# First layer of a feed-forward block as seven block products for five more token chunks, with the whole schedule laid anew

## The chip, the cores and the metric

The kernel runs on one core of a Trainium2 chip. The core has a matrix engine (PE, with its own row for weight loads, PEld), a vector engine (DVE), a scalar engine for exp, log and copies (ACT), a general engine (POOL) which here mostly issues loads, and SP, which issues stores and DMA transposes. Each engine gets its own list of instructions, in the order in which the kernel issues them; between engines semaphores make one wait for another. In this kernel PE's results go to banks of PSUM, from which ACT and DVE read; all other tiles lie in SBUF. The metric is device time in microseconds from start to end of one launch.

## The reference

Attention with 8 heads over 4 batches of 768 positions, head size 64, followed by a feed-forward block on the 3072 x 512 result:

```python
scores = scale * np.matmul(q, k.transpose(0, 1, 3, 2)) + bias     # bias = -slope * distance
scores = np.where(is_global | is_local, scores, -1e9)             # 8 global keys, 96 local ones
a = softmax(scores)
x = (a @ v).transpose(0, 2, 1, 3).reshape(3072, 512)
h = x @ w_in                                                      # 512 -> 2048, layer 1
g = np.maximum(h, 0.0) + np.log1p(np.exp(-np.abs(h)))             # softplus
return g @ w_out                                                  # 2048 -> 512, layer 2
```

The output is float32, 3072 x 512.

## The kernel before

Tokens are worked in 24 blocks of 128 (six a batch) for attention and in 12 chunks of 256 (two blocks each) for the feed-forward block. A block needs, for the local window, its own keys and those of the block before it; the eight global keys are copied into the unused rows of the latter (`gk`, `gv`).

For a block n the steps are: loads of q, k and v on POOL's queue, which cast to bf16 (`lq`, `lk`, `lv`); transposes of q and k, in the first blocks on PE with copies out of PSUM (`t`, `qc`, `kc`), from block 8 on by DMA from SP's queue (`d`); scores (`s`, or `ss` for both halves of the heads); the bias added on DVE (`ab`, `ac`; in the first blocks by a matmul, `z`); exp on ACT (`e`); PV (`p`); division by the sum on DVE (`nm`); transposition of the result (`x` with its copy `xc`, or `y` by DMA), which gives `XT`, the input of layer 1.

Layer 1 of a chunk c has two forms. In the direct one, for chunks 0 to 6, it is eight units `f`, numbered 8c + u, each of two output blocks of 128 features and four contraction steps, that is eight matmuls of 128 x 128 by 256 columns (`ffn1`, L429), into one of three rotating PSUM banks. ACT takes an exp of each unit (`fe`, `soft`, L440), and a log of 1 + that for two units together (`lp`, `plus`, L448), which gives G, the input of layer 2.

In the other form, for chunks 7 to 11, the product is split in two along features in, features out and tokens, and made of seven block products instead of eight (Strassen, in Winograd's arrangement). Each half u of the blocks runs through: product 1 into bank "x" (`h`, `h_prod`, L536, eight matmuls by 128 columns); a copy of x into bank "y" (`hc` 1, `h_copy`, L546); product 2 added into y, which is output quarter 11; product 5 into bank "z", copied to SBUF as `hp` (`hc` 5, L549); product 6 added into x; z = hp + x on DVE (`hv` 6, `h_sum`, L561); product 3 added into z, quarter 12; product 7 added into x; quarter 22 = hp + x, on DVE into SBUF (`hv` 7); product 4 added into x, quarter 21. Each quarter then gets its exp (`he`, `h_exp`, L566), each half of the features its log (`hl`, `h_plus`, L570). The differences of the input are made on DVE (`ht`, `x_dif`, L507), the sums of the weights once, in eight parts (`hw`, `w_sum_part`, L480 to L490). Between product 1 and the last exps such a unit holds three banks, x, y and z.

The same three banks, b0, b1 and b2, serve the transposes on PE and half of the scores (`s_lo`); which of them each user gets stands in the string BANKS. The other banks are fixed: two for scores, one for PV, two for layer 2.

Layer 2 of chunks 1 to 11 is made of seven block products too (`m`, `prod`, L652), eight matmuls by 256 columns each, with sums of G on DVE (`gs`, L622) and copies and sums out of PSUM (`ec`, L681; `ev`, L691). Chunk 0 has it direct (`o`, L581). Stores (`st`) go by SP's queue.

What sets the order of all work is written out by hand: the string ORDER lists every step once, and a loop calls them in that order, so each engine, each DMA queue and each PSUM bank gets its work as the string has it. Steps of the kind `g` (L700) are copies of one element of G on POOL, which hold back the loads behind them until that part of G is there. `w18` is nine matmuls on constants at the start.

```python
    for name in ORDER.split():
        kind = name.rstrip("0123456789.")
        KINDS[kind](*(int(i) for i in name[len(kind) :].split(".")))
```

## Time and profile before

| what | value |
|---|---|
| timed runs | 203.88, 204.22, 205.57 us; median 204.22 |
| profiled execution, first to last instruction (span) | 201.9 us |
| median of the timed runs above that span | 2.3 us |
| PE busy | 195.3 us, 97% |
| weight loads (PEld) busy | 166.9 us, 83% |
| DVE busy | 163.6 us, 81% |
| ACT busy | 163.4 us, 81% |
| POOL busy | 77.0 us, 38% |
| granted TensorE clock | 1.000 |
| direct layer 1: matmuls | 448, mean 273 ns |
| seven-product layer 1: matmuls | 560, mean 219 ns |

The page gives the profiled execution by its span alone; its own time beside the span is not among the records, so the median of the timed runs stands in the table. A group's row has its line, engine, operation, output and inputs, shapes and count, then the busy time and the mean of one, then the idle time of the engine just before and what ended it. Matmuls overlap: the mean of one is its latency, and how many fit into a stretch is seen from start to start in the timeline. The slices of the page are 40 equal parts of the span, each about 5 us.

### The profile page before, as it was taken

Reading aid. Unit: us, or ns where it says so; the run is one execution under the profiler, and the core shown is the slowest. Engines: PE = TensorE matmul, PEld = TensorE weight load, DVE = VectorE, ACT = ScalarE, POOL = GpSimd, SP = SyncE. Lnnn points to the kernel's source line nnn. Section 1 sums busy time; section 2 is a strip of 40 time slices with the busy share of each in tenths; the row PEclk is TensorE's granted clock in tenths of the full one; section 3 lists DMA queues with packets and bytes.
Section 4 is the critical chain, followed back from the end, with each engine's and each line's share of the span. In section 5 each row is a group of like instructions: output and inputs, shape, how many; then the busy total and the mean of one; then the engine's idle time right before and its main releaser. Section 6 shows DMA issues by size and latency. Waiting matters only on the chain.

```text
span 201.9 us, 6147 instructions
## 1 busy us (share of the span) xinstructions
PE 195.3 (97%) x2487; PEld 166.9 (83%) x2489; DVE 163.6 (81%) x392; ACT 163.4 (81%) x253; POOL 77.0 (38%) x119
## 2 busy tenths in 40 slices
PE   7899999999999999999999998999999999999993
...
DVE  7765479589999988787889989999999986888541
ACT  2976899936599799687897998999999898999410
...
PEclk9999999999999999999999999999999999999999
...
GB/s 129 152 169 175 162 190 191 205 164 151 169 116 126 134 204 110 148 143 127 133 193 161 197 89 155 154 141 160 162 117 108 29 52 81 0 109 0 3 208 104
DMA packets 110619, 26.87 MB, mean 133 GB/s; under 512 B 101760, under 2 KB 108288, under 8 KB 110592
## 3 DMA queue, kind: packets, MB, share of 16 engines
...
q10 hardware_dynamic: 1040, 0.26, 0.6%
...
## 4 chain that ended last, share of the span: by engine, by line
PE 79%; DMA 7%; ACT 6%; DVE 5%; issue 1%; DVEq 0%; ACTq 0%
PE o L652 28%; PE hT L429 23%; PE hT L536 8%; PE x_ps L375 4%; PE s_ps L279 3%; PE o L581 3%; DMA out_dram<-osb 3%; PE p_ps L536 3%; ACT Pb L359 3%; DMA k_f<-in_k_dram 2%; DMA XT<-xsf 2%; PE tr L222 2%; ACT e_sb L566 2%; PE s_lo L279 1%; ACT G L570 1%
## 5 line engine op out<-in xcount | busy, mean ns | idle before, releaser
L429 PE MATMUL hT<-XT,w_in 128*128 128x256 f16 x448 | 56.2, 273 | 0.0
L429 PEld LDWEIGHTS <-w_in 128*128 128x128 f16 x448 | 41.8, 98 | 6.3
L359 ACT ACTIVATE Pb<-Z 128x1024 bf16<-128x1024 f32 (+1 forms) x40 | 39.2, 990 | 3.8 <-DVE Z L339 1.7
L440 ACT ACTIVATE e_sb<-hT 128x512 f32<-128x512 f32 x56 | 32.0, 594 | 10.6 <-PE hT L429 10.3
L652 PEld LDWEIGHTS <-sum 128*128 128x128 f16 x352 | 33.2, 98 | 4.3 <-issue 0.3
L652 PE MATMUL o<-w_dif,sum 128*128 128x256 f16 x264 | 33.9, 273 | 0.1
L700 POOL CAST gate_t<-G 1x1 bf16<-1x1 f16 x32 | 6.9, 214 | 68.6 <-ACT G L448 34.9
L448 ACT ACTIVATE G<-e_sb 128x1024 f16<-128x1024 f32 x28 | 29.2, 1062 | 0.2
L652 PEld LDWEIGHTS <-G 128*128 128x128 f16 x272 | 25.0, 98 | 2.8
L100 POOL DMA_DIRECT2D k_t<-in_k_dram x23 | 20.6, 898 | 16.1 <-DMA KT<-k_t 14.6
L339 DVE TENSOR_TENSOR Z<-s_ps,biasA 128x1024 f32<-128x1024 f32 x19 | 23.1, 1216 | 3.6 <-PE s_ps L279 3.4
L100 POOL DMA_DIRECT2D v_t<-in_v_dram x24 | 21.8, 910 | 1.1 <-issue 0.6
L100 POOL DMA_DIRECT2D q_t<-in_q_dram x23 | 20.8, 907 | 2.3 <-DMA w_in<-in_moe_w_in_dram 1.6
L652 PE MATMUL o<-w_out,G 128*128 128x256 f16 x168 | 21.6, 273 | 0.0
L570 ACT ACTIVATE G<-e_sb 128x1024 f16<-128x1024 f32 x20 | 20.9, 1064 | 0.2
L536 PEld LDWEIGHTS <-w_sum 128*128 128x128 f16 x320 | 19.7, 98 | 1.0 <-issue 0.5
L393 DVE TENSOR_TENSOR xsf<-x_ps,rcp 128x256 f16<-128x256 f32 x44 | 18.7, 424 | 1.5
L375 PEld LDWEIGHTS <-Pb 128*128 128x128 bf16 x352 | 16.1, 98 | 2.5 <-ACT Pb L359 0.9
L375 PE MATMUL x_ps<-v_t,Pb 128*128 128x65 bf16 x324 | 17.1, 193 | 0.1
L622 DVE TENSOR_TENSOR sum<-G 128x1024 f16<-128x1024 f16 x22 | 15.0, 682 | 1.8 <-ACT G L448 1.4
L536 PEld LDWEIGHTS <-w_in 128*128 128x128 f16 x240 | 14.7, 98 | 1.1 <-issue 0.5
L279 PEld LDWEIGHTS <-KT 64*128 64x128 bf16 x352 | 9.9, 94 | 5.2 <-issue 3.6
...
## 6 DMA issues: line engine op xcount, KB each, us to landing
...
w_out<-in_moe_w_out_dram POOLq DMA_DIRECT2D x4, 512.0 KB, 12.4
...
w_in<-in_moe_w_in_dram POOLq DMA_DIRECT2D x2, 512.0 KB, 8.9
```

The costliest lines, as they stand in the source:

```text
L100: nc.gpsimd.dma_start(dst[n][:, :, 0:D], src[b, :, i * P : (i + 1) * P, :].rearrange("h s d -> s h d"))
L279: nc.tensor.matmul(dst(4 * sub + 2 * mm + t), KT[n - t][rows, m, :], QT[n][rows, m, :], start=not pre and not (whole and (t or mm)), stop= ...
L339: nc.vector.tensor_tensor(Z[:], buf[:, 0:8, :], biasA[:, half, :, :], ALU.add)
L359: nc.scalar.activation(Pb[:, 0:nreg, :], src, AF.Exp, scale=inv_sqrt)
L375: nc.tensor.matmul(x_b[:, lh, :], Pb[:, r, :], v_t[n - t][:, h, :], start=(t == 0), stop=(t == 1 or first),)
L393: nc.vector.tensor_tensor(xsf[:, h0 : h0 + 4, :], x_b[:, :, 0:D], rcp[:, h0 : h0 + 4][:, :, None].to_broadcast([P, 4, D]), ALU.mult,)
L429: nc.tensor.matmul(hT[:, j, :], w[:, m, fo : fo + P], XT[c][:, m, :], start=(j == 0 and m == 0), stop=(m == KM - 1), skip_group_check=(j > 0),
L440: nc.scalar.activation(ES[c, u // 2][:, j : j + 2, :], HT.pop((c, u))[:], AF.Exp)
L448: nc.scalar.activation(g_tile(c)[:, 4 * w : 4 * w + 4, :], ES.pop((c, w))[:], AF.Ln, bias=1.0)
L536: nc.tensor.matmul(o[:, b, :], lhs(k, b), rhs[:, k, :], start=(i in (1, 5) and b == 0 and k == 0), stop=(k == KH - 1), skip_group_check=True,)
L570: nc.scalar.activation(g_tile(c)[:, b0 : b0 + HB, :], HS.pop((c, i, u))[:], AF.Ln, bias=1.0)
L652: nc.tensor.matmul(o, lhs[:, k, :], rhs(k)[:, c0:c1], start=(i in (1, 2, 5) and k == 0), stop=(k == NU - 1), skip_group_check=(i not in (1 ...
```

## The change

Chunks 2 to 6 (tokens 512 to 1791) get layer 1 as seven block products too, as chunks 7 to 11 have it; only chunks 0 and 1 remain direct. No function of the arithmetic is new. The 40 direct units with their 40 exps and 20 logs give way to 70 block products, 20 copies (all marked for ACT), 20 sums, 20 differences, 40 exps and 20 logs. All steps in ORDER stand in a new order, the loads among them; the string BANKS has 116 entries in place of 126. Steps of the kinds `gk` and `gv` for the first two blocks of a batch do nothing, wherever they stand. Two conditions in `norm` and `tr_x` now ask whether a tile is there yet, so that the halves of a block and the blocks of a chunk may come in either order.

```diff
--- before.py
+++ after.py
@@ -184,8 +184,8 @@
 
 
     BANKS = iter(
-        "01201201202012012012012020120210212021012012201202120210120120120100210102102120"
-        "2101202120100120201012020212120110220110221001"
+        "01201201201201021202102021202010120200020111201200212210101022210110220211211010"
+        "020201012212022010102001221010202121"
     )
 
     def any_bank(shape, dtype, name):
@@ -380,7 +380,7 @@
 
     def norm(n, half):
         x_b = XB.pop((n, half))
-        if half == 0:
+        if n not in xt:
             xt[n] = (
                 work.tile([P, H, D], F16, tag="xsf", name="xsf"),
                 work.tile([P, H], F32, tag="rcp", name="rcp"),
@@ -397,7 +397,7 @@
 
     def tr_x(n, by_dma=False):
         xsf, _ = xt.pop(n)
-        if n % 2 == 0:
+        if n // 2 not in XT:
             XT[n // 2] = xtp.tile([P, NPAIR, CT], F16, tag="XT", name="XT")
         dst = XT[n // 2][:, :, P * (n % 2) : P * (n % 2) + P]
         if by_dma:
@@ -700,75 +700,91 @@
         nc.gpsimd.tensor_copy(gate_t[:], G[c][0:1, 2 * u + 1, 0:1])
 
     ORDER = """
-        w18 bb1.0 cq0 ck0 bb0.0 lq1 tq0 lk1 tk0 lv0 z0.0 lk2 z0.1 s0.0 bb0.1 e0.0 lq2 bb1.1 t1 qc1.0
-        kc1.0 lv1 s0.1 e0.1 lq3 lk3 z1.0 p0.0 s1.0 p0.1 z1.1 s1.1 e1.0 e1.1 nm0.0 t2 nm0.1 x0 z2.0
-        gk2 p1.0 p1.1 qc2.0 lv2 kc2.0 nm1.0 s2.0 lv3 xc0.1 nm1.1 z2.1 s2.1 wi2 wi3 e2.0 gv2 x1 t3
-        qc3.0 e2.1 kc3.0 wi0 z3.0 p2.0 nm2.0 p2.1 gk3 lk4 s3.0 z3.1 gv3 s3.1 nm2.1 x2 e3.0 e3.1 p3.0
-        xc1.0 xc2.0 p3.1 gk4 f2 fe2 f3 fe3 lp1 nm3.0 nm3.1 x3 f0 fe0 xc3.0 f10 lq4 t4 qc4.0 fe10 f8
-        fe8 wi1 f9 wi4 gv4 kc4.0 s4.0 ab4.0 fe9 lp4 f1 f11 fe1 s4.1 lk5 f4 lq5 t5 ab4.1 fe11 e4.0
-        e4.1 f12 fe12 qc5.0 gk5 kc5.0 lv4 p4.0 s5.0 wi6 f5 nm4.0 lp0 ab5.0 lv5 fe4 p4.1 gv5 nm4.1
-        e5.0 f13 fe5 fe13 lp5 s5.1 wo0 f6 fe6 hw3.0 ab5.1 p5.0 x4 xc4.0 gs1.3 nm5.0 hw1.0 lk6 f7 o0
-        f14 f15 e5.1 lq6 p5.1 wo1 fe7 lp6 wo2 t6 nm5.1 fe14 wd1.0 wo3 o4 x5 lp3 g7 xc5.0 o1 fe15 lq7
-        lk7 lk8 qc6.1 lq8 f18 o5 f16 lp2 o2 lv6 wd1.1 kc6.0 o6 wd3.0 f19 lp7 fe16 gs1.1 fe18 gs1.2
-        wd2.0 wd4.0 gs1.4 o7 os0.1 o3 wd2.1 ss6 fe19 f17 lq9 lv7 lk9 fe17 t7 os0.0 m1.1.0 ab6.0 e6.0
-        ac6.0 lp9 ac6.1 e6.1 qc7.0 f22 kc7.0 lq10 d8 p6.0 lv8 ss7 g15 lk10 wd3.1 lk12 f20 nm6.0 p6.1
-        ab7.0 fe22 ec1.1.1 e7.0 m1.6 ac7.0 nm6.1 f21 ac7.1 x6 xc6.0 ec1.6.1 p7.0 m1.2.1 d9 nm7.0
-        m1.7 gk8 ev1.2 wd4.1 e7.1 p7.1 gv8 nm7.1 ec1.7.1 fe20 fe21 ss8 m1.4 ab8.0 x7 lk11 ec1.4.1
-        f23 e8.0 ac8.0 lq11 xc7.0 gk9 ac8.1 m1.5.0 ev1.5 p8.0 nm8.0 lp8 gs2.3 f24 lv9 e8.1 d10 fe24
-        m1.3 ev1.3 fe23 lp11 lp10 p8.1 gv9 nm8.1 ss9 ab9.0 ac9.1 gk10 ac9.0 lk13 lv10 f28 f29 fe28
...
-        lp25 f49 fe53 e17.0 fe48 fe49 e17.1 ec5.6.0 gv17 nm16.1 m5.7 ht7.1 ht7.3 lv17 st3.0 ht7.2
-        ht7.4 st3.1 p17.0 d18 nm17.0 ec5.7.1 h7.1.0 hc7.1.0.0 lp24 d19 y16 m5.5.1 ev5.5 h7.5.0 p17.1
-        nm17.1 y17 gs6.3 hc7.5.0.1 h7.2.0 he7.11.0 g51 m5.3 ev5.3 h7.6.0 hv7.6.0 lv18 ss18 ab18.0
-        lp26 h7.7.0 h7.3.0 ac18.1 ac18.0 hv7.7.0 e18.0 he7.12.0 ss19 e18.1 he7.22.0 p18.0 gk18
-        h7.4.0 he7.21.0 ab19.0 h7.1.1 ac19.0 hc7.1.1.1 ac19.1 m5.4 e19.0 h7.5.1 lk20 lq20 nm18.0 g35
...
-        hl11.1.0 gs10.4 m9.5.1 m10.6 hv11.7.1 hl11.0.0 he11.11.1 h11.4.1 he11.12.1 hl11.0.1 ec10.6.1
-        ev9.5 gs11.3 m9.3 st8.1 ev9.3 he11.21.1 m10.7 ec10.7.0 m9.2.1 ev9.2 he11.22.1 hl11.1.1
-        gs11.1 gs11.2 m11.2.2.1 st8.0 m10.4 ec10.4.1 m10.5.1 ev10.5 gv19 m11.1.0 ec11.1.1 m10.3
-        m11.6 ev10.3 gs11.4 m10.2.1 ec11.6.1 ev10.2 m11.7 ec11.7.0 st10.1 st9.1 m11.5.1 st9.0 ev11.5
-        m11.4 m11.3 st10.0 ec11.4.1 ev11.2.1 ev11.3 st11.1 st11.0.1 m11.2.2.0 ev11.2.0 st11.0.0 gv13
+        cq0 wi4 bb1.0 w18 ck0 lk1 tq0 z0.1 bb1.1 lq1 tk0 s0.1 z0.0 lk2 bb0.1 s0.0 e0.1 bb0.0 lq2
+        e0.0 z1.1 t1 kc1.0 lv0 lv1 qc1.0 z1.0 lk3 s1.0 t2 s1.1 e1.0 p0.1 qc2.0 p0.0 gk2 kc2.0
+        nm0.0 z2.0 s2.0 e1.1 p1.0 nm0.1 p1.1 z2.1 lq3 s2.1 lk4 t3 e2.0 lv2 nm1.1 lq4 nm1.0 z3.0
+        wi1 gv2 lv3 x0 qc3.0 wi0 e2.1 gk3 x1 kc3.0 xc0.1 z3.1 xc1.0 s3.1 s3.0 e3.1 gk4 p2.1 t4
+        nm2.1 wi2 kc4.0 e3.0 p2.0 f5 qc4.0 gv3 wi3 f4 fe4 lq5 fe5 nm2.0 p3.0 nm3.0 s4.0 x2 p3.1
+        f1 lp2 f0 hw1.0 xc2.0 f2 fe0 nm3.1 fe1 ab4.0 e4.0 hw3.0 gk18 x3 s4.1 f3 lv4 xc3.0 gv4
+        hw2.0 fe2 ab4.1 hw4.0 lp0 fe3 f8 fe8 lk5 wi6 p4.0 e4.1 wo0 f9 t5 lv5 f10 nm4.0 kc5.0 gk5
+        lp1 fe10 qc5.0 fe9 hw3.1 p4.1 lp4 wo2 s5.0 f11 ab5.0 f7 gv5 wo1 fe7 f6 fe11 hw1.1 nm4.1
+        s5.1 wo3 f13 lk6 hw2.1 o0 ab5.1 wd1.0 e5.0 x4 fe13 p5.0 xc4.0 e5.1 fe6 lp5 hw4.1 lq6
+        nm5.0 lv6 f15 f14 lp3 p5.1 wd2.0 f12 o4 nm5.1 wd3.0 gs1.3 wd4.0 wd1.1 o5 lq7 fe14 x5
+        fe12 o1 xc5.0 wd2.1 fe15 ht2.1 lp7 lp6 h2.1.0 wd4.1 wd3.1 hc2.1.0.1 ht2.2 lq8 o6 ht2.3
+        o7 gs1.1 h2.2.0 os0.1 t6 he2.11.0 h2.6.0 qc6.1 g7 kc6.0 h2.5.0 lk7 ss6 gs1.2 ht2.4 o2
+        hc2.5.0.1 lk8 ac6.0 hv2.6.0 ab6.0 t7 lv11 h2.3.0 e6.0 qc7.0 h2.7.0 o3 ac6.1 he2.12.0 g15
+        kc7.0 hv2.7.0 lv7 p6.0 lv12 d8 os0.0 ss7 e6.1 ac7.0 h2.4.0 h2.5.1 lk9 gv19 nm6.0 h2.1.1
+        lv10 lq9 hl2.0.0 ab7.0 he2.21.0 m1.1.0 d9 gv13 hc2.1.1.1 ac7.1 lk11 hc2.5.1.1 h2.6.1
+        p6.1 lk10 hv2.6.1 nm6.1 ec1.1.1 gk8 e7.0 h2.2.1 m1.2.1 gs1.4 he2.11.1 h2.7.1 ev1.2 p7.0
+        hv2.7.1 m1.6 he2.22.0 e7.1 ec1.6.1 nm7.0 ss8 m1.7 gk9 he2.22.1 h2.3.1 hl2.1.0 ec1.7.1
+        lv13 ac8.0 he2.12.1 p7.1 ab8.0 lv8 gv8 h2.4.1 x6 nm7.1 e8.0 lq11 m1.4 ac8.1 xc6.0
+        he2.21.1 x7 xc7.0 p8.0 nm8.0 e8.1 ec1.4.1 lv9 ss9 hl2.1.1 ht3.1 ac9.0 h3.1.0 p8.1 ht3.2
+        h3.5.0 lq13 m1.5.0 ab9.0 hc3.1.0.1 hc3.5.0.1 hl2.0.1 h3.6.0 ev1.5 st0.1 h3.2.0 ht3.3
+        hv3.6.0 ac9.1 m1.3 h3.3.0 ev1.3 he3.11.0 h3.7.0 lk13 st0.0 e9.0 nm8.1 lk12 lq10 ht3.4
+        hv3.7.0 h3.1.1 m2.1.0 d11 h3.4.0 gv9 he3.12.0 e9.1 d10 hc3.1.1.1 he3.21.0 gs2.1 p9.0
+        ec2.1.0 lq12 h3.2.1 gs2.2 h3.5.1 nm9.0 he3.11.1 hc3.5.1.1 gs2.3 h3.6.1 hl3.0.0 hv3.6.1
+        gk10 p9.1 m2.6 lq14 ec2.6.1 gv10 h3.7.1 nm9.1 ss10 hv3.7.1 y8 he3.22.0 ab10.0 m2.7 y9
+        ec2.7.0 lq15 gk11 h3.4.1 h3.3.1 hl3.1.0 ac10.0 ac10.1 he3.22.1 gs2.4 e10.0 he3.12.1
+        ht4.1 d12 m2.4 ec2.4.1 h4.1.0 lk14 ss11 m2.5.0 d13 he3.21.1 ht4.2 g21 ac11.0 hc4.1.0.1
+        st1.1 ac11.1 h4.6.0 h4.5.0 gk19 e10.1 h4.2.0 hl3.0.1 hc4.5.0.1 ht4.3 g27 ev2.5 ab11.0
+        p10.0 he4.11.0 m2.2.1 m2.3 hl3.1.1 hv4.6.0 e11.1 h4.7.0 nm10.0 h4.3.0 ev2.2 ss12 ev2.3
+        hv4.7.0 p10.1 he4.12.0 m3.1.0 he4.22.0 g23 d14 ht4.4 h4.4.0 e11.0 gs3.1 ec3.1.1 he4.21.0
+        st1.0 ac12.0 h4.5.1 nm10.1 gv11 h4.1.1 hc4.1.1.1 p11.0 gs3.2 ac12.1 lk16 m3.6 hc4.5.1.1
+        h4.2.1 h4.6.1 g13 ab12.0 nm11.0 e12.0 he4.11.1 gs3.3 p11.1 ec3.6.1 ss13 hv4.6.1 h4.3.1
...
+        ec8.4.0 he10.21.0 gs9.3 st7.0 m9.1.1 p23.1 hc10.1.1.0 nm23.1 hl9.1.1 h10.5.1 hc10.5.1.1
+        gs9.1 ec9.1.1 h10.6.1 hv10.6.1 h10.2.1 m8.5.0 h10.7.1 gs9.2 he10.11.1 hv10.7.1 h10.3.1
+        y23 m9.6 ec9.6.0 ht11.1 h10.4.1 h11.1.0 hl10.0.0 hl10.1.0 ht11.2 he10.12.1 st7.1
+        he10.21.1 hc11.1.0.1 m9.7 ht11.3 h11.5.0 gs9.4 h11.6.0 hc11.5.0.1 ev8.5 hv11.6.0
+        hl10.0.1 ht11.4 ec9.7.0 h11.2.0 m8.3 gs10.3 he11.11.0 ev8.3 h11.7.0 h11.3.0 m9.4 m10.1.0
+        hv11.7.0 he10.22.1 ec9.4.0 he11.12.0 st8.0 ec10.1.0 hl10.1.1 h11.4.0 he11.21.0 gs10.1
+        g69 m9.5.1 h11.1.1 hc11.1.1.1 g67 gs10.2 ev9.5 h11.5.1 he11.22.0 m10.6 h11.6.1
+        hc11.5.1.1 hl11.1.0 h11.2.1 he11.11.1 ec10.6.1 m9.3 hl11.0.0 st8.1 hv11.6.1 h11.7.1
+        ev9.3 hv11.7.1 h11.3.1 he11.22.1 m10.7 ec10.7.0 gs10.4 h11.4.1 he11.12.1 he11.21.1
+        m9.2.1 ev9.2 hl11.0.1 m10.4 m10.5.1 ec10.4.1 m11.1.0 hl11.1.1 ev10.5 st9.0 ec11.1.1
+        st10.1 st9.1 gs11.1 m10.3 m11.2.2.0 gs11.2 m11.2.2.1 gs11.3 m11.6 ec11.6.1 ev10.3
+        m10.2.1 m11.7 gs11.4 ev10.2 st10.0 m11.5.1 ec11.7.0 ev11.5 ev11.2.0 m11.4 ec11.4.1 m11.3
+        ev11.2.1 ev11.3 st11.0.1 st11.1 st11.0.0
```

84 lines of the change are left out of this document (41 added, 43 removed).

## The prediction

> **What bounds the kernel now.** I read the page first: shares of each engine, then the slices.
>
> ```profile
> span 201.9 us, 6147 instructions
> ...
> PE 195.3 (97%) x2487; PEld 166.9 (83%) x2489; DVE 163.6 (81%) x392; ACT 163.4 (81%) x253; POOL 77.0 (38%) x119
> ...
> PE   7899999999999999999999998999999999999993
> ...
> DVE  7765479589999988787889989999999986888541
> ACT  2976899936599799687897998999999898999410
> ...
> PEclk9999999999999999999999999999999999999999
> ...
> GB/s 129 152 169 175 162 190 191 205 164 151 169 116 126 134 204 110 148 143 127 133 193 161 197 89 155 154 141 160 162 117 108 29 52 81 0 109 0 3 208 104
> ```
>
> PE is in work nearly all the time, at full granted clock, so shorter PE work should shorten the span. But DVE and ACT are full too in the middle, at 80% on average only because start and end are thin. An average hides that, so the second view is busy time by stretch.
>
> ```profile
> core 0: us, PE busy (x) PEld busy (x) DVE busy (x) ACT busy (x) POOL busy (x), PEclk, DMA share, GB/s
> 20.00:120.00 100.00, 99.85 (x1180) 84.40 (x1178) 84.11 (x190) 83.44 (x122) 46.03 (x68) 1.00 1.56 155
> 120.00:140.00 20.00, 19.30 (x308) 17.80 (x306) 18.88 (x42) 18.95 (x32) 9.62 (x17) 1.00 1.82 151
> 140.00:190.00 50.00, 49.82 (x724) 46.31 (x721) 42.67 (x95) 46.44 (x74) 3.08 (x9) 1.00 0.42 72
> ```
>
> ```profile
> 140.00:150.00 10.00, 10.00 (x173) 9.10 (x170) 9.69 (x26) 9.52 (x17) 2.55 (x6) 1.00 1.33 151
> 150.00:160.00 10.00, 10.00 (x156) 9.24 (x155) 9.49 (x20) 9.95 (x17) 0.00 (x0) 1.00 0.28 72
> ```
>
> From 20 to 120 us, where layer 1 is direct and DVE and ACT are at 84%, PE is idle 0.15 us in 100. From 120 to about 160 seven-product layer 1 runs beside the last six blocks of attention: DVE 18.88 + 9.69 + 9.49 = 38.1 of 40 us, 95%, ACT 38.4, 96%. There PE loses 0.70 us, all of it before 140: 3.5% of that half, 1.75% of the whole. The third view, the chain that ended last, says who takes it there:
>
> ```profile
> 122.26 0.46 PE hT L536 x8
> 122.81 0.69 DVE p_ps L561
> ...
> 136.97 0.60 DVE e_sb L561
> 137.61 1.05 PE hT L536 x16
> ```
>
> Before 122 and after 138 the chain runs mostly along PE; between these rows it runs along DVE and ACT, entered and left at the block sums of L561. The 40 us from 120 are a sample of what the change makes of the middle of the kernel.
>
> **The PE saving.** A recorded matmul outlasts the time to the next one, so I take pitches from the timeline.
>
> ```profile
> 101.95 1.04 PE L429 MATMUL hT<-XT,w_in 128*128 128x256 f16 x8
> 102.82 1.04 PE L652 MATMUL o<-w_dif,G 128*128 128x256 f16 x8
> ...
> 131.08 0.61 PE L536 MATMUL p_ps<-XT,w_sum 128*128 128x128 f16 x8
> 131.52 0.61 PE L536 MATMUL hT<-XT,w_in 128*128 128x128 f16 x8
> 131.97 0.61 PE L536 MATMUL hT<-x_dif,w_in 128*128 128x128 f16 x8
> ```
>
> A direct unit of layer 1 (one `f`, eight matmuls of 256 columns) takes 102.82 - 101.95 = 0.87 us; a block product (one `h`, eight matmuls of 128 columns) 131.97 - 131.08 over two = 0.445 us. A chunk needs eight `f` or fourteen `h`: 6.96 against 6.23 us, 0.73 us less. Five chunks: **-3.65 us**. Everything else on PE (QK, PV, layer 2, transposes) has the same count before and after.
>
> A rule speaks against this. The Trainium skill, "TensorE: Matmul & The Clock Gate", section "Back-to-back issue gap", gives about 81 ns per matmul of 128 columns in a real stream of weight loads and matmuls. By that estimate fourteen `h` would cost 112 x 81 ns = 9.1 us a chunk, and five chunks would come out about 10.6 us longer, not 3.65 shorter. This trace disagrees: 0.445 us for eight is 56 ns each.
>
> **What DVE and ACT get in addition.** Per chunk four differences of x (`ht`), four PSUM copies (`hc`; all 20 new ones are marked for ACT), four sums (`hv`). The eight exps and four logs remain eight and four.
>
> ```profile
> L440 ACT ACTIVATE e_sb<-hT 128x512 f32<-128x512 f32 x56 | 32.0, 594 | 10.6 <-PE hT L429 10.3
> ...
> L566 ACT ACTIVATE e_sb<-e_sb 128x512 f32<-128x512 f32 x10 | 6.4, 635 | 0.0
> ```
>
> ```profile
> 124.68 0.68 DVE L561 TENSOR_TENSOR e_sb<-hp,hT 128x512 f32<-128x512 f32 x1
> 125.27 1.22 DVE L339 TENSOR_TENSOR Z<-s_ps,biasA 128x1024 f32<-128x1024 f32 x1
> ...
> 133.16 0.28 DVE L507 TENSOR_TENSOR x_dif<-XT,x_dif 128x256 f16<-128x256 f16 x1
> 133.37 0.18 DVE L390 RECIPROCAL rcp<-x_ps 128x4 f32<-128x4 f32 x1
> ```
>
> ```profile
> 140.81 0.59 ACT L549 COPY hp<-p_ps 128x512 f32<-128x512 f32 x1
> 141.27 0.40 ACT L681 COPY u<-o 128x256 f32<-128x256 f32 x1
> ```
>
> Start to start a sum takes 0.59 us, a difference 0.21, a copy on ACT 0.46. So DVE gets 20 x 0.59 + 20 x 0.21 = 16.0 us, ACT 20 x 0.46 = 9.2 us and about 0.5 us for exps (a quarter of the 40 at 635 instead of 594 ns), 9.7 in all. By the stretches DVE has 84.11 + 18.88 + 42.67 = 145.7 us in the 170 us from 20 to 190, ACT 148.8. With the additions, in a stretch shorter by 3.65 us: DVE 161.7 of 166.3, 97%; ACT 158.5, 95%. So nothing here lies on the path as long as its queue keeps up, but both queues lose nearly all their slack, and the three engines run for most of the kernel as full as now from 120 to 160.
>
> Added waits: `h2` and `h6` wait for the copy `hc1`, `h3` and `h7` for the sum `hv6`, `h4` for `hv7`. Behind each in PE's queue stand layer 2 products (`m`), PV and QK of the next block, which then wait too, and ACT waits for their results. A unit of four outputs also takes all three rotating PSUM banks, where `f` took one until its exp; transposes and half of the QK of later blocks want the same three.
>
> **What that costs** the trace of before doesn't show for the new order, so I bound it. Low end: nothing lost, as from 140 to 160 (10.00 and 10.00). High end: the loss of 120 to 140. The busy row hides short gaps, since a recorded matmul of 219 ns covers any gap up to 0.16 us behind its pitch, so that 3.5% may really be twice as much, 7%. Attention and seven products overlap in the new order from `h2.1.0` to `p23.1`. With the pitches above `h2.1.0` comes about 40 us into the work and `p23.1` about 160: 120 us. Blocks 6 to 23 are spread over them, 6.7 us a block, against 6.7 for the six blocks of the sample's 40 us. The mix is the same, so I take the sample's rate, 1.75%, and a little for the gaps that the row hides: 2%, 2.4 us. What is lost now goes away: 0.70 + 0.15 + 0.18 = 1.0. Net **+1.4 us** (between -1.0 and +7.4).
>
> **The start.** `wi4`, so far the seventeenth load on POOL's queue, becomes the first, ahead of `lk1`, `lq1`, `lv0`.
>
> ```profile
> w_in<-in_moe_w_in_dram POOLq DMA_DIRECT2D x2, 512.0 KB, 8.9
> ...
> 7.16 0.40 PE L222 MATMUL tr<-ident,q_t 128*128 128x128 bf16 x4
> ...
> 17.34 1.91 PE L429 MATMUL hT<-XT,w_in 128*128 128x256 f16 x16
> ```
>
> At the 152 to 175 GB/s of the second to fourth slice its 512 KB hold the queue 3.0 to 3.4 us, so block 1's transposes, now at 7.16, may start some 3 us later, and each later load of the start comes as much later. Against it: the first `f` (17.34 now, after all of block 3) needs `wi4` and blocks 0 and 1 alone, and stands ahead of `p3.0`, so PE has work while block 3 is still in ACT's exps; the other weights and blocks are in by then at that rate. Bounds -0.5 (two PV groups moved behind) and +3.0; I take 0, since the `f` work fills what block 3 leaves open. The eight `w_sum` sums, all pulled ahead of `h2.1.0`, fall between 20 and 40 us, where DVE's slices show 4 to 9 tenths; with no such cover they would be 5 us more on DVE. The gates on POOL and the DMA transposes keep their number; POOL is at 38%. The last layer 2 products end in the same way as now.
>
> **Sum.** The profiled execution has a span of 201.9 us; the median of the timed runs is 204.22, 2.3 us of which lie around the span and don't change. 204.2 - 3.65 + 1.4 + 0 = **202.0 us**.
>
> **Rivals.**
> - *Nothing lost* (DVE at 97% still runs ahead of PE): -3.65 and up to -1.0 for today's gaps, 199.5 to 201. For it: from 45 to 70 us DVE's and PE's slices are all at 9. Against it: three engines above 95% with three banks between them. Chance 0.14.
> - *Gain eaten*: the visible loss of 120 to 140 throughout, 3.5% of 120 us = 4.2, less 1.0, or the late start's 3.0: 204.2 - 3.65 + 3.2 = 203.7; 203 to 206. Chance 0.18.
> - *Slower*: the chain hc1, h6, hv6, h7, hv7 through three banks, with ACT's and DVE's queues full, sets the pace of the whole middle. At 7% of 120 us 8.4 are lost: 204.2 - 3.65 + 7.4 = 207.9. It decides from (3.65 + 1.0) / 120 = 3.9% on; 1% slower than before needs 5.6%. For it: the chain from 122.81 to 137.61. Chance 0.24.
> - *Weight loads bound PE at 128 columns*: if each of 112 loads took its own 98 ns, a chunk would take 11.0 us and the kernel 20 us more, 222.
>
> ```profile
> L536 PEld LDWEIGHTS <-w_sum 128*128 128x128 f16 x320 | 19.7, 98 | 1.0 <-issue 0.5
> ```
>
> The same row speaks against it: 19.7 us for 320 is 62 ns each, so loads overlap, and the products already run at 56 ns. (The 81 ns of the Trainium skill, quoted above, belong to this rival.) Chance 0.02.
>
> That the change does something else than it says I leave out: the new order has 70 more `h`, 40 less `f`.
>
> **Chances and range.** The forecast, 201 to 203, has 0.42. Within 1% (202.2 to 206.3) is about what a measurement can tell from no change. Faster: two thirds of the forecast and the first rival, 0.28 + 0.14 = 0.42. Same: the rest of it and the second, 0.32. Slower: 0.26. The range from 200.0 to 207.6 takes in the forecast, most of the first rival, the second, and the third up to a loss of 6.7%.
>
> **What would show it.** Right: 40 `f` of 0.87 us fewer and 70 `h` of 0.445 us more in PE's timeline; DVE busy near 180, ACT near 173; PE busy still above 97% of a span near 199.7; the chain along PE. Wrong: between 40 and 160 us a PE busy below 96%, the chain on L561 and L549 for long, waits of PE and its weight loads for DVE or ACT; the first `f` later than 18 us; block products slower than 0.45 us.

## The result, and the profile after

The changed kernel takes 218.22 us (median; 215.56 to 218.8) beside 204.37 us for the kernel before (203.88 to 205.57) on the same chip: a ratio of 1.064, 95% interval 1.056 to 1.072. It is slower by 13.9 us; the forecast of 202.0 and its range miss that on the wrong side. The profiled execution has a span of 216.2 us where before's had 201.9. Here and below, times are medians over all runs, while ratios and intervals leave out the runs that lay more than 1.5% above the fastest of their kernel.

The page of the changed kernel: span, busy times, slices, and the first line of the chain that ended last.

```profile
span 216.2 us, 6679 instructions
...
PE 197.0 (91%) x2727; PEld 169.1 (78%) x2729; DVE 177.1 (82%) x432; ACT 174.1 (81%) x273; POOL 77.1 (36%) x119
...
PEclk9769999999999999999999999799999999999999
...
PE 52%; DMA 24%; DVE 12%; ACT 4%; POOL 3%; issue 3%; SPq 1%; DVEq 0%; POOLq 0%; ACTq 0%
```

The same line of the chain on the page of the kernel before:

```profile
PE 79%; DMA 7%; ACT 6%; DVE 5%; issue 1%; DVEq 0%; ACTq 0%
```

DVE and ACT have the work that was forecast (177.1 and 174.1 us; near 180 and 173 were said). The chain is another one: PE had 79% of it before and 52% now, DMA 7% before and 24% now, DVE and ACT together 11% and 16%. Now the same stretches of both kernels. The columns are the stretch, its length, then busy time and count for PE, PEld, DVE, ACT and POOL, granted clock, DMA share and GB/s; the first fence is before, the second after.

```profile
0.00:20.00 20.00, 17.68 (x206) 10.79 (x209) 13.49 (x57) 13.12 (x24) 18.31 (x27) 1.00 1.74 156
20.00:60.00 40.00, 40.00 (x447) 31.96 (x445) 31.63 (x68) 31.33 (x46) 21.79 (x28) 1.00 1.73 169
60.00:160.00 100.00, 99.16 (x1363) 88.58 (x1362) 90.55 (x208) 90.54 (x140) 36.41 (x62) 1.00 1.39 140
```

```profile
0.00:20.00 20.00, 16.35 (x164) 8.95 (x167) 11.25 (x49) 11.11 (x20) 14.78 (x22) 0.83 1.65 148
20.00:60.00 40.00, 38.91 (x491) 31.25 (x488) 37.03 (x86) 32.85 (x51) 25.80 (x32) 1.00 1.82 166
60.00:160.00 100.00, 88.95 (x1374) 80.09 (x1371) 86.16 (x203) 87.09 (x137) 34.18 (x57) 0.98 1.28 132
```

From 60 to 160 us PE is idle for 11 us in 100, DVE and ACT are less busy than before in the same stretch, and the first 20 us run at a granted clock of 0.83. Busy time hides what stands between short matmuls, so for every kernel below I also take the *lost time*: for each recorded matmul the time from its start to the next one's start, less the pitch of its form at full clock (56 ns at 128 columns, 109 at 256, 216 at 512, 28 for QK, 29 for PV). The sum of the pitches is the *work*, that is, counts times pitches. (The nine matmuls on constants at the start, slower in every kernel, are counted as work at the time they took, about 2 us more.) All figures are us of the profiled execution, one for each kernel.

| kernel | work | lost | 0-30 | 30-60 | 60-160 | later |
|---|---|---|---|---|---|---|
| before | 186.2 | 11.5 | 5.0 | 0.9 | 5.2 | 0.4 |
| after | 182.6 | 29.1 | 8.6 | 2.1 | 17.9 | 0.5 |

Work fell by 3.6 us. The loss rose by 17.6: 3.6 at the start, 1.2 from 30 to 60, 12.7 from 60 to 160. Together that is 14.0 of the 14.3 us by which the span grew. The loss from 60 to 160 is not a steady rate: single gaps of 0.6 to 2.0 us, at 61.9, 73.7, 80.8, 94.2, 111.5, 117, 131 and 148 us, make up 12.5 of its 17.9 us (gaps of over 0.3 us; before 1.4 of 5.2). Waits of the changed kernel (engine, line, what it waited for; total us, times, longest):

```profile
POOL q_t L100 <- DMA QT<-q_t: 28.1, 4, 9.8
DVE x_dif L507 <- DMA XT<-xsf: 5.8, 3, 2.2
PE s_ps L279 <- DMA KT<-k_t: 3.2, 2, 1.8
PE hT L536 <- DMA XT<-xsf: 1.6, 1, 1.6
PE x_ps L375 <- DMA v_t<-in_v_dram: 1.2, 2, 0.9
```

In the first, POOL's queue stands at a load whose tile a transpose has not read yet. Before had 14.6 us of that kind:

```profile
POOL k_t L100 <- DMA KT<-k_t: 14.6, 2, 7.7
```

The four others aren't among before's waits at all. Followed one by one in the timeline, the gaps at 80.8, 94.2, 111.5 and 131 us (6.6 us together) stand behind transposes of x, those at 61.9 and 73.7 (3.5) behind transposes of k, that at 117 (1.3) behind a store, that at 148 (1.1) behind a load of v. This is the gap at 111.5 us in the timeline of the changed kernel:

```profile
105.78 1.81 SPq L404 DMA_TRANSPOSE XT<-xsf  x1
...
112.28 0.29 DVE L507 TENSOR_TENSOR x_dif<-XT 128x256 f16<-128x256 f16 x1 [2.21 <-DMA XT<-xsf]
112.49 0.68 DVE L348 TENSOR_TENSOR Z<-s_lo,biasA 128x512 f32<-128x512 f32 x1
113.23 0.61 PE L536 MATMUL p_ps<-x_dif,w_sum 128*128 128x128 f16 x8 [1.51 <-DVE Z L348]
```

The transpose of a finished block of x (`y`) is issued at 105.78. DVE stands at the difference that reads it (`ht`) until 112.28, 6.5 us after that issue; the bias sums of the next scores stand behind it in DVE's queue, and PE then waits 1.51 us. So the first question was whether late transfers are the whole of the loss.

### The profile page after: what moved, and what is told of

The parts are those of the page before. It is cut to its first block, busy times and chain, and to the rows that moved or that the text cites. A ratio compares the mean times of both kernels' runs of the same rounds, so it can differ in the third digit from the quotient of the medians.

```text
span 216.2 us, 6679 instructions
## 1 busy us (share of the span) xinstructions
PE 197.0 (91%) x2727; PEld 169.1 (78%) x2729; DVE 177.1 (82%) x432; ACT 174.1 (81%) x273; POOL 77.1 (36%) x119
## 4 chain that ended last, share of the span: by engine, by line
PE 52%; DMA 24%; DVE 12%; ACT 4%; POOL 3%; issue 3%; SPq 1%; DVEq 0%; POOLq 0%; ACTq 0%
PE o L652 20%; PE hT L536 13%; DMA XT<-xsf 6%; PE p_ps L536 5%; DMA w_in<-in_moe_w_in_dram 4%; DMA q_t<-in_q_dram 3%; DMA out_dram<-osb 3%; PE o L581 3%; PE x_ps L375 3%; DMA KT<-k_t 3%; DVE Z L339 3%; DMA QT<-q_t 3%; DMA v_t<-in_v_dram 2%; PE s_ps L279 2%; DVE Z L348 2%
## 5 line engine op out<-in xcount | busy, mean ns | idle before, releaser
L536 PEld LDWEIGHTS <-w_sum 128*128 128x128 f16 x640 | 39.4, 98 | 4.9 <-DVE x_dif L507 2.0
L570 ACT ACTIVATE G<-e_sb 128x1024 f16<-128x1024 f32 x40 | 42.0, 1059 | 0.0
L536 PEld LDWEIGHTS <-w_in 128*128 128x128 f16 x480 | 29.3, 98 | 3.3 <-DMA XT<-xsf 1.9
L566 ACT ACTIVATE e_sb<-hT 128x512 f32<-128x512 f32 x40 | 23.9, 599 | 4.3 <-PE hT L536 3.2
L536 PE MATMUL hT<-XT,w_in 128*128 128x128 f16 x320 | 24.4, 219 | 1.6 <-DMA XT<-xsf 1.6
L536 PE MATMUL hT<-x_dif,w_sum 128*128 128x128 f16 x320 | 24.4, 219 | 0.8 <-DVE x_dif L507 0.8
L375 PEld LDWEIGHTS <-Pb 128*128 128x128 bf16 x352 | 15.7, 99 | 4.5 <-issue 2.4
L279 PEld LDWEIGHTS <-KT 64*128 64x128 bf16 x352 | 10.3, 96 | 10.4 <-DMA KT<-k_t 3.5
L561 DVE TENSOR_TENSOR p_ps<-hp,hT 128x512 f32<-128x512 f32 x20 | 13.8, 689 | 2.7 <-PE hT L536 1.8
L429 PE MATMUL hT<-XT,w_in 128*128 128x256 f16 x128 | 15.6, 273 | 0.3 <-DMA w_in<-in_moe_w_in_dram 0.3
## 6 DMA issues: line engine op xcount, KB each, us to landing
w_out<-in_moe_w_out_dram POOLq DMA_DIRECT2D x4, 512.0 KB, 12.5
```

The lines of the kernel that those rows point to most:

```text
L279: nc.tensor.matmul(dst(4 * sub + 2 * mm + t), KT[n - t][rows, m, :], QT[n][rows, m, :], start=not pre and not (whole and (t or mm)), stop= ...
L375: nc.tensor.matmul(x_b[:, lh, :], Pb[:, r, :], v_t[n - t][:, h, :], start=(t == 0), stop=(t == 1 or first),)
L429: nc.tensor.matmul(hT[:, j, :], w[:, m, fo : fo + P], XT[c][:, m, :], start=(j == 0 and m == 0), stop=(m == KM - 1), skip_group_check=(j > 0),
L536: nc.tensor.matmul(o[:, b, :], lhs(k, b), rhs[:, k, :], start=(i in (1, 5) and b == 0 and k == 0), stop=(k == KH - 1), skip_group_check=True,)
L561: nc.vector.tensor_tensor(t, HS[c, "p", u][:], HT[c, "x", u][:], ALU.add)
L566: nc.scalar.activation(o, t, AF.Exp)
```

## Experiments

The theory after this reading: **T**, transfers come back too late for steps that now stand closer behind them, and the new start. Its rivals: **Q**, my own, DVE, ACT and three banks are too full and hold PE; **P**, the seven products themselves cost more than the direct form.

### Is it the seven products, or the places of the loads?

The four kernels of this group differ from the changed one in ORDER alone (and in the bank string where steps change).

loads_by_use, at chunk 2 (the same steps, the loads dealt anew over their places):

```diff
-        fe12 o1 xc5.0 wd2.1 fe15 ht2.1 lp7 lp6 h2.1.0 wd4.1 wd3.1 hc2.1.0.1 ht2.2 lq8 o6 ht2.3
...
-        hc2.5.0.1 lk8 ac6.0 hv2.6.0 ab6.0 t7 lv11 h2.3.0 e6.0 qc7.0 h2.7.0 o3 ac6.1 he2.12.0 g15
-        kc7.0 hv2.7.0 lv7 p6.0 lv12 d8 os0.0 ss7 e6.1 ac7.0 h2.4.0 h2.5.1 lk9 gv19 nm6.0 h2.1.1
+        os0.1 t6 he2.11.0 h2.6.0 qc6.1 g7 kc6.0 h2.5.0 lq8 ss6 gs1.2 ht2.4 o2 hc2.5.0.1 lk8 ac6.0
+        hv2.6.0 ab6.0 t7 lk9 h2.3.0 e6.0 qc7.0 h2.7.0 o3 ac6.1 he2.12.0 g15 kc7.0 hv2.7.0 lq9 p6.0
+        lv7 d8 os0.0 ss7 e6.1 ac7.0 h2.4.0 h2.5.1 lv8 gv19 nm6.0 h2.1.1 lk11 lq11 hl2.0.0 ab7.0
```

wi4_later:

```diff
-        cq0 wi4 bb1.0 w18 ck0 lk1 tq0 z0.1 bb1.1 lq1 tk0 s0.1 z0.0 lk2 bb0.1 s0.0 e0.1 bb0.0 lq2
...
-        nm0.0 z2.0 s2.0 e1.1 p1.0 nm0.1 p1.1 z2.1 lq3 s2.1 lk4 t3 e2.0 lv2 nm1.1 lq4 nm1.0 z3.0
+        cq0 bb1.0 w18 ck0 lk1 tq0 z0.1 bb1.1 lq1 tk0 s0.1 z0.0 lk2 bb0.1 s0.0 e0.1 bb0.0 lq2 e0.0
...
+        z2.0 s2.0 e1.1 p1.0 nm0.1 p1.1 z2.1 lq3 wi4 s2.1 lk4 t3 e2.0 lv2 nm1.1 lq4 nm1.0 z3.0 wi1
```

direct_again, for chunks 2 to 6:

```diff
-        fe12 o1 xc5.0 wd2.1 fe15 ht2.1 lp7 lp6 h2.1.0 wd4.1 wd3.1 hc2.1.0.1 ht2.2 lq8 o6 ht2.3
-        o7 gs1.1 h2.2.0 os0.1 t6 he2.11.0 h2.6.0 qc6.1 g7 kc6.0 h2.5.0 lk7 ss6 gs1.2 ht2.4 o2
+        wd2.1 fe15 lp7 lp6 f16 fe16 wd4.1 wd3.1 lq8 o6 o7 gs1.1 os0.1 t6 f20 fe20 qc6.1 g7 kc6.0
+        f17 fe17 lk7 ss6 gs1.2 o2 lk8 ac6.0 ab6.0 t7 lv11 e6.0 qc7.0 f21 fe21 o3 ac6.1 g15 kc7.0
```

loads_sp_by_use is loads_by_use with the DMA transposes laid anew too: each `y` right behind its block's division, each `d` in the order of blocks.

> The changed kernel with one thing different: the loads of q, k and v stand in the order of their use, in the same places of the order text; compute order, DMA transposes, stores and gates as they were. Late loads (the chain of the changed kernel runs through KT<-k_t at 57.6 us, QT<-q_t at 76.4 and v_t at 143.9, behind loads that POOL's queue has to hold): the gaps of 1.5, 2.0, 1.0 and 1.1 us at 62, 74, 81 and 148 us go, 4 to 8 us off 218.2, 210 to 214. Queues of DVE and ACT with three PSUM banks as the limit: the loads were not what ended last, 217 to 219.

> The same, and the DMA transposes on SP's queue re-laid too: each XT<-xsf right behind its division, those of q and k in the order of the blocks. Late transfers: the gaps before block products at 94, 111 and 131 us (1.8, 1.7, 0.8 and 1.4 us, chain XT<-xsf) shrink as well, 3 to 5 us more off, 205 to 210. Queues of DVE and ACT: 217 to 219.

> The changed kernel's order with chunks 2 to 6 direct again: each pair of block products gives way to direct units in the same places, their exps right behind them, banks dealt anew; loads, transposes, stores, attention and layer 2 stand where they stood. Late transfers: they stay late, and PE gets 3.65 us more work: 217 to 222. Queues of DVE and ACT with three banks: 16 us of DVE, 9.7 of ACT and two of three banks of each unit are free again, 205 to 209.

> The changed kernel with the first weight load (wi4) put behind the loads of q and k of block 3, nothing else. The start as one cost by itself: PE lost 8.6 us in the first 30 against 5.0 before; with q and k of block 1 first on the queue again 2.5 to 3.5 us come back, 214.7 to 215.7. If the start's loss is hidden behind something later: 217.5 to 218.5.

| kernel | us | ratio to before (95%) | work | lost | 0-30 | 60-160 |
|---|---|---|---|---|---|---|
| loads_by_use | 215.66 | 1.054 (1.047 to 1.061) | 183.1 | 27.0 | 8.9 | 15.4 |
| loads_sp_by_use | 220.07 | 1.068 (1.057 to 1.080) | 183.1 | 31.1 | 7.9 | 21.0 |
| direct_again | 220.79 | 1.080 (1.073 to 1.088) | 186.6 | 27.3 | 8.1 | 16.0 |
| wi4_later | 215.89 | 1.054 (1.046 to 1.062) | 183.1 | 25.7 | 8.6 | 14.6 |

direct_again decides against P: with the direct form back in the new order, nearly the whole loss stays, and the work that the products had saved is added. It speaks against Q as well. Its stretch from 60 to 160 us:

```profile
60.00:160.00 100.00, 91.96 (x1172) 78.48 (x1170) 74.12 (x169) 77.94 (x118) 34.41 (x57) 0.98 1.33 132
```

DVE is at 74% there and ACT at 78%, well below the 90% of the kernel before, and PE still loses 16.0 us. Loads in order of use, and `wi4` later, give back 2.6 and 2.3 us of the median, no more than the runs of the changed kernel scatter (215.56 to 218.8), and their intervals overlap its interval. `wi4` later also does not do what was expected of it: its start loses the same 8.6 us as the changed kernel's (PE there waits 2.8 us for a load of v that now stands behind `wi4`), and its gain lies between 60 and 160 us. Transposes put earlier in ORDER bring nothing: by the ratios the kernel is some 3 us slower than loads_by_use, with intervals that just overlap, where 3 to 5 us less were expected. In its trace, as in the changed kernel's, SP issues the `y` of nearly every block at the very end of that block's division (0.0 us behind it for 12 of 16 blocks), so that an earlier place brings nothing.

### More room for the transfers by moving layers 1 and 2 back

late_h25 moves layer 1 and layer 2 of chunks 4 to 9 later by 2.5 us of PE work against attention; all_h25 adds the two repairs of the loads, all_h4 moves by 4 us. loads_no_gates is loads_by_use without the gates `g` on POOL.

late_h25, at chunk 7 (BANKS is dealt anew):

```diff
-        ab19.0 hv7.6.1 h7.7.1 h7.3.1 h7.2.1 nm18.0 e19.0 hv7.7.1 gs6.1 st5.1 gk20 g57 p18.1 y17
-        st4.0 he7.12.1 he7.11.1 ht8.1 h7.4.1 lv19 ev5.2 ht8.2 h8.1.0 ec6.1.1 he7.21.1 h8.5.0
+        he7.21.0 h7.1.1 h7.5.1 ab19.0 m6.1.0 g45 g55 hc7.1.1.1 h7.6.1 nm18.0 e19.0 gk20 p18.1 y17
+        hc7.5.1.1 m5.2.1 lv19 hl7.0.0 he7.22.0 hv7.6.1 h7.7.1 nm18.1 h7.3.1 h7.2.1 hv7.7.1 gs6.1
+        st5.1 g57 he7.12.1 he7.11.1 ht8.1 h7.4.1 st4.0 d22 ht8.2 h8.1.0 ev5.2 e19.1 d21 p19.0 y18
```

> The changed kernel with one thing different: layer 1 and layer 2 of chunks 4 to 9 come 2.5 us of PE's work later against attention, which gives each DMA transpose XT<-xsf that much more time before its first block product; loads as in the changed kernel, banks dealt anew. If the missing room between transposes and their users is the cause: the gaps of 1.8, 1.7, 0.8 and 1.4 us before block products at 94 to 132 us shrink, 2 to 5 us off 218.2, 213 to 216. If the transposes are late for whatever room they have, because of the loads: 217 to 219.

> The three repairs together: the first weight load behind the loads of q, k and v of blocks 1 to 3, loads in the order of use, layer 1 and 2 of chunks 4 to 9 later by 2.5 us. If the three causes add up: 218.2 less 2.3 (start), 2.5 (loads) and 2 to 5: 208 to 212. If DVE's, ACT's and the banks' limit stands right behind them: 213 to 216.

> The same with 4 us instead of 2.5. If room before the first block product is what lacks: another 1 to 3 us off, 205 to 210. If the queues of DVE and ACT set the pace by now: no better than with 2.5 us, within 1.5 us of it.

> Loads in the order of use, and the gates on POOL (one-element copies of G that hold the loads behind them) left out; nothing else. If the gates make loads late: below 213. If it is the transposes' room that lacks, loads that come earlier only crowd the transposes: 214.5 to 218.

late_h25 took 251.25 us (ratio 1.232, 1.226 to 1.237), all_h25 247.46 (1.207), all_h4 255.69 (1.259); loads_no_gates 216.13 (1.060, 1.055 to 1.065), the same as with gates. All three that move layers are 29 us or more worse than the changed kernel. The stretches of late_h25 from 60 us on:

```profile
60.00:160.00 100.00, 79.13 (x1114) 68.70 (x1112) 73.28 (x169) 71.37 (x110) 32.14 (x52) 0.93 1.16 111
160.00:200.00 40.00, 34.15 (x482) 29.54 (x479) 29.64 (x66) 31.13 (x49) 3.75 (x13) 0.96 0.48 70
```

It loses 17.9 us after 160 us too, where the changed kernel loses 0.5. Moving whole chunks against each other changed much more than the room of the transfers, and the loss went to stretches without transfers too. So their times say nothing for or against T. Their waits say more. In late_h25 the time from the issue of the transpose of a chunk's second block to its first reader is 5.7 to 11.6 us for chunks 4 to 11 (in the changed kernel 3.7 to 6.5), and only one difference still waits for a transpose, 2.9 us; in all_h4 it is 5.9 to 12.8 us and none does. So with more room those waits go. What comes in their place is PE waiting for DVE and ACT, in late_h25 above all for the block sums:

```profile
PE hT L536 <- DVE e_sb L561: 7.0, 9, 1.9
```

That is the mechanism of Q, in a worse order. How the 29 us and more add up isn't shown.

### Nobody waits for the late tiles

The next kernels leave every step in its place and change which tile is read. The tiles that stay get buffers of their own, so that the rings of `XT`, `QT` and v have one or two buffers fewer for the others; fix_all_before has the same edits and shows what they cost by themselves. Excerpts (fix_x: x; fix_qkv: q, k, v; fix_all both; fix_all_before the same in the kernel before):

```diff
-                    hT[:, j, :], w[:, m, fo : fo + P], XT[c][:, m, :],
+                    hT[:, j, :], w[:, m, fo : fo + P], XT[min(c, 3)][:, m, :],
-                        dst(4 * sub + 2 * mm + t), KT[n - t][rows, m, :], QT[n][rows, m, :],
+                        dst(4 * sub + 2 * mm + t), KT[min(n, 7) - t][rows, m, :], QT[min(n, 7)][rows, m, :],
-                    x_b[:, lh, :], Pb[:, r, :], v_t[n - t][:, h, :],
+                    x_b[:, lh, :], Pb[:, r, :], v_t[min(n, 7) - t][:, h, :],
```

> The changed kernel, in which layer 1 of chunks 4 to 11 reads the input of chunk 3, which has long been there, in place of its own; the DMA transposes XT<-xsf run as ever, but nobody waits for them. Left out: the outputs of chunks 4 to 11 are those of other tokens. Order, engines' work and banks are unchanged. Late transfers as the cause: the gaps before block products at 94, 111 and 131 us go, 4 to 7 us off 218.2, 211 to 214. Queues of DVE and ACT with three banks: 216 to 219.

> The changed kernel, in which the scores and PV of blocks 8 to 23 read q, k and v of blocks 6 and 7 in place of their own, so nobody waits for the loads of later blocks and their DMA transposes, which run as ever; the copies of the global keys go to unused tiles. Left out: attention of blocks 8 to 23 with their own data. Late transfers: the gaps at 62, 74 and 148 us and part of the others go, 4 to 8 us off, 210 to 214. Queues of DVE and ACT: 216 to 219.

> Both: no compute step from block 8 and chunk 4 on waits for a load or a DMA transpose (stores remain). Left out: as in the two before. Late transfers as the whole cause in the middle: the 13 us that PE loses between 60 and 150 us beyond the kernel before go, the start's 3.6 stay: 203 to 207. Queues of DVE and ACT with three banks: 212 or more.

> The same two edits on the kernel before, as a measure: what the waits for loads and transposes cost there. Both theories: 0 to 2 us off, 202 to 204.5. Left out: as above.

fix_x took 215.35 us (1.052, 1.043 to 1.060), fix_qkv 216.32 (1.060, 1.054 to 1.065), fix_all 213.70 (1.043, 1.035 to 1.051), fix_all_before 203.66 (0.999, 0.997 to 1.002). Only 4.5 of the 13.9 us came back, and I took that for a sign of Q. The timeline of fix_all says otherwise:

```profile
96.78 0.42 DVE L400 TENSOR_TENSOR xsf<-x_ps,rcp 128x256 f16<-128x256 f32 x1 [4.46 <-DMA XT<-xsf]
...
97.26 0.29 PE L382 MATMUL x_ps<-v_t,Pb 128*128 128x65 bf16 x4 [3.57 <-DVE xsf L400]
```

Nobody reads XT any more, but its transfer still has to read `xsf` before DVE may write the next block there, and DVE stands 4.46 us for that, PE behind it 3.57. The kernel had taken away the readers' waits and left the writers'. A second way by which the same late transfer stops the same engine had been overlooked.

### The transfers left out

no_moves is fix_all with the loads of q, k and v (`lq`, `lk`, `lv`) and the transposes by DMA (`d`, `y`) from block 8 on struck from ORDER; no_moves_start also has `wi4` behind `lq3 lv2`; no_moves_before strikes the same steps from fix_all_before. no_loads strikes only the loads, from the changed kernel with all its reads, so that the later blocks work on old data; no_transposes strikes only `d` and `y`, from fix_all. both_repairs computes everything and joins the two repairs:

```diff
-        cq0 wi4 bb1.0 w18 ck0 lk1 tq0 z0.1 bb1.1 lq1 tk0 s0.1 z0.0 lk2 bb0.1 s0.0 e0.1 bb0.0 lq2
...
+        z2.0 s2.0 e1.1 p1.0 nm0.1 p1.1 z2.1 lq3 lv2 wi4 s2.1 lk4 t3 e2.0 nm1.1 lq4 nm1.0 z3.0 wi1
```

and no_moves, at blocks 8 and 9:

```diff
-        gk10 p9.1 m2.6 lq14 ec2.6.1 gv10 h3.7.1 nm9.1 ss10 hv3.7.1 y8 he3.22.0 ab10.0 m2.7 y9
+        hv3.7.1 he3.22.0 ab10.0 m2.7 ec2.7.0 gk11 h3.4.1 h3.3.1 hl3.1.0 ac10.0 ac10.1 he3.22.1
```

> As fix_all, and the transfers that nobody reads any more are not issued: no loads of q, k and v and no DMA transposes of q, k and x from block 8 on. So the scores, PV and layer 1 of the later blocks and chunks work on kept tiles, and most of the output is not the reference's. Every step of TensorE, VectorE and ScalarE and every bank stays where it is in the changed kernel. In fix_all one gap of 3.7 us at 93.5 us stands behind VectorE, which waits 4.46 us to write xsf until an earlier XT<-xsf transfer has read it: that can't happen here. Theory A (late transfers and the new start are all of it): the kernel before's 203.7 less 3.65 of work, and 3 to 4 for the start, 203 to 205.5 us. Theory B (the order of the engines' own steps, three banks, DVE and ACT at 80%): 210 to 213 us, near fix_all's 213.7.

> no_moves with the load of wi4 moved behind lq3 and lv2 (four steps of POOL's queue later than q, k and v of blocks 0 to 2). Theory A: 200 to 202.5 us, which is the forecast of 202.0. Theory B: 207 to 211 us.

> The same transfers left out of the kernel before, which left out nothing in time when its late tiles were replaced (203.66): 202 to 204 us by both theories. It is the base that no_moves is compared with.

> The changed kernel, with the loads of q, k and v from block 8 on not issued; their DMA transposes and those of x are, in the same places, and everything that reads them waits for them as before, so the later blocks work on what the ring's slots held. If the transposes are late because the loads fill the DMA engines (q0 had 88 to 93% of them) or because their q and k come late: 205 to 207.5 us, like no_moves, and XT<-xsf lands in well under the 3.6 us of the median now. If the transposes are late by their own places in SP's queue: 211 to 215 us.

> fix_all with the loads of q, k and v kept and the DMA transposes of q, k and x from block 8 on not issued: nobody waits for a transpose, and the loads of q and k wait for nobody. If the loads harm only through the transposes that wait for them or run beside them: 205 to 207 us, like no_moves. If loads hold engines by themselves (PV of an earlier block must be done with v's slot, and POOL's queue holds the gates and weights behind it): 208 to 212 us.

> The changed kernel, everything computed, with wi4 behind lq3 and lv2 (wi4_later gave 215.89, and had put wi4 ahead of lv2) and the loads of q, k and v in the order of their use (215.66). If the two parts add up: 212.5 to 214 us. If the gaps only move: 215 to 216.5 us.

| kernel | us | ratio to before (95%) | work | lost | 0-30 | 30-60 | 60-160 |
|---|---|---|---|---|---|---|---|
| fix_all | 213.70 | 1.043 (1.035 to 1.051) | 183.1 | 24.8 | 10.3 | 1.8 | 12.2 |
| no_moves | 205.37 | 1.004 (1.000 to 1.008) | 183.1 | 15.8 | 8.9 | 2.3 | 4.5 |
| no_moves_start | 204.13 | 0.998 (0.994 to 1.002) | 183.1 | 15.7 | 9.2 | 1.9 | 4.5 |
| no_moves_before | 204.10 | 1.000 (0.998 to 1.003) | 186.6 | 11.5 | 5.1 | 1.1 | 4.9 |
| no_loads | 208.77 | 1.020 (1.010 to 1.030) | 182.6 | 20.0 | 8.3 | 7.1 | 4.6 |
| no_transposes | 206.47 | 1.011 (1.004 to 1.018) | 182.6 | 18.5 | 10.3 | 2.1 | 6.1 |
| both_repairs | 212.63 | 1.033 (1.024 to 1.041) | 183.1 | 20.5 | 6.0 | 1.6 | 12.6 |

Leaving out the transfers gives back 12.9 us of the changed kernel's time (218.22 to 205.37) and nothing of before's. From 60 to 160 us no_moves loses 4.5 us, less than before's 5.2. What keeps it at 205.37, and not near the forecast of 202.0, is mostly the start, 8.9 us to 30 us beside 5.1 in no_moves_before. no_moves_start was to mend that (200 to 202.5 us were expected) and did not: it loses 9.2 us there, now with a wait of 3.2 us for the q of block 4, which stands behind `wi4`. The same stretch of no_moves, and then of no_loads:

```profile
60.00:160.00 100.00, 99.76 (x1584) 91.75 (x1583) 98.41 (x233) 99.01 (x158) 6.00 (x30) 1.00 0.10 35
```

```profile
60.00:160.00 100.00, 99.87 (x1591) 91.63 (x1588) 98.35 (x236) 99.00 (x159) 5.35 (x27) 1.00 0.41 84
```

PE, DVE and ACT are busy for 99.8, 98.4 and 99.0 us of the same 100, and nothing is lost beside before. Both kernels keep every engine's order of the compute steps, and no_loads keeps the real reads of the x, q and k tiles. So Q falls for this order: full queues and three banks carry seven products beside attention without added loss as long as no transfer is late.

no_loads and no_transposes say which transfers. With the loads gone and each transpose in its place, nobody waits for a transpose. The next three lines are the times from issue to landing of the transposes of x, in the kernels before, after and no_loads:

```profile
DMA to landing us min/median/max: 2.4/4.4/6.1
```

```profile
DMA to landing us min/median/max: 2.4/3.6/7.2
```

```profile
DMA to landing us min/median/max: 2.4/2.4/3.9
```

With the transposes gone and the loads kept, the loss from 60 to 160 is 6.1 us. Neither kind does much harm alone; together they do. The Trainium skill, "DMA: Bandwidth & Descriptors", section "Issuing engines are not separate DMA queues", says that transfers started by different engines run on the same 16 DMA engines and interleave. The rows agree: loads go by POOL's queue, transposes by SP's, and striking the first shortens the second. What these runs don't part is that no_loads also has q and k there early.

But the transposes of x took as long in the kernel before. The medians above hide that: the last six of the changed kernel are issued from 149 us on, when hardly a load is left, and land in 2.4 to 2.7 us; the ten before them take 2.4 to 7.2, some 5 us in the middle, where before's up to 150 us take 2.4 to 6.1, 4.8 in the middle. What the kernel before had was room. From the issue of the transpose of a chunk's second block to the first difference that reads it, before has 9.2 to 11.4 us for chunks 7 to 11; the changed kernel, its waits included, 3.7 to 6.5 us for chunks 4 to 11. Two examples, the second blocks of chunk 9 before (146.23 - 134.94 = 11.3) and of chunk 7 after (131.14 - 124.97 = 6.2, of which DVE waits 2.07):

```profile
134.94 1.23 SPq L404 DMA_TRANSPOSE XT<-xsf  x1
...
146.23 0.49 DVE L507 TENSOR_TENSOR x_dif<-XT 128x256 f16<-128x256 f16 x2
```

```profile
124.97 1.32 SPq L404 DMA_TRANSPOSE XT<-xsf  x1
131.14 0.29 DVE L507 TENSOR_TENSOR x_dif<-XT 128x256 f16<-128x256 f16 x1 [2.07 <-DMA XT<-xsf]
131.49 0.62 PE L536 MATMUL p_ps<-x_dif,w_sum 128*128 128x128 f16 x8 [0.62 <-DVE x_dif L507]
```

Since SP issues these transposes when the division ends, the room is the distance from a block's division to its chunk's layer 1, and the new order has shortened that. In no_loads the same distance is 3.6 to 4.9 us, and with 2.4 to 3.9 us to land that is enough; with up to 7.2 it is not.

both_repairs leaves that distance as it is. In its profiled execution (209.82 us, the fastest of its four) the start is nearly back (6.0 us lost to 30 us; before 5.0), though no_moves_start, with the same loads ahead of `wi4`, still lost 9.2; its stretch from 60 to 160 is not (12.6), and the second line of its chain shows why:

```profile
PE o L652 19%; PE hT L536 11%; DMA XT<-xsf 10%; PE hT L429 6%; DVE Z L348 5%; PE p_ps L536 4%; PE o L581 3%; DMA v_t<-in_v_dram 3%; DVE sum L622 3%; DVE xsf L393 3%; PE x_ps L375 3%; DVE p_ps L561 2%; DVE Z L339 2%; PE s_ps L279 2%; DVE osb L691 2%
```

It is the fastest version with everything computed in the new order, 5.6 us better than the change as made, and 3% slower than the kernel before.

What stays open: no_loads loses 7.1 us from 30 to 60, where the changed kernel loses 2.1. One wait there is 2.1 us of layer 2 of chunk 0 for a load of `w_out`, and its granted clock from 40 to 50 us is 0.83; why that load came later without the others, the runs don't tell. Nor does any run show an order that gives the transposes their old room and keeps the rest. That late transfers cost the 12.9 us is shown by no_moves; that it is the lost room that makes those of x late is argued from these rows, from no_loads and from the waits that went in late_h25 and all_h4, not shown by a faster kernel. And the x transposes account for about half of the gaps alone; for those behind the transposes of k, the store and the load of v there are only no_moves and no_loads, in which they go too.

## Why the prediction was wrong

- **The PE saving held.** -3.65 us was said; work fell by 3.6 (186.2 to 182.6). Work is counts times pitches, so this is the forecast's own sum unless the pitch held. It did: block products that follow one another in the changed kernel start 0.445 us apart.

```profile
103.33 0.61 PE L536 MATMUL p_ps<-XT,w_sum 128*128 128x128 f16 x8
103.77 0.61 PE L536 MATMUL hT<-x_dif,w_in 128*128 128x128 f16 x8
104.22 0.61 PE L536 MATMUL hT<-XT,w_in 128*128 128x128 f16 x8
```

The rival of weight loads that bind the products falls with these rows. The 81 ns per matmul of the Trainium skill, "TensorE: Matmul & The Clock Gate", section "Back-to-back issue gap", do not hold here either: at 81 instead of 56 ns the 560 added matmuls of 128 columns would have raised the work by 14 us.

- **DVE and ACT held in amount**: busy 177.1 and 174.1 us where near 180 and near 173 were said.
- **The coupling of DVE, ACT and three banks was over-priced, and the third rival had the wrong mechanism.** Taken at +1.4 us, bounds -1.0 to +7.4. With no late transfers the loss from 60 to 160 is 4.5 us, against 5.2 before. The chain by L561 and L549, my only mechanism for a slower kernel, did not take PE's time in this order, so the chance of 0.24 that a slower kernel got there stood on the wrong reason. (In late_h25 that chain does hold PE.) The sample of 120 to 140 us that the price came from was a fair sample of compute, and hence of nothing that mattered.
- **The step that failed** is the half sentence "the gates on POOL and the DMA transposes keep their number", which put the transfers at nothing. Their number stayed, and so did, while loads run, their time (4.8 us before and some 5 after for x, in the middle); the distance from the issue to the first reader fell from 9 to 11 us to some 4 to 6.5. The term that was put at nothing came to 12.9 us: that is what no_moves gives back, and 12.7 is the growth of the loss from 60 to 160. About half of it stands behind transposes of x, the rest behind those of k, a store and a load of v, and up to 1.7 us of it is the granted clock (0.83 from 130 to 140 us), which fell just behind such a gap. It could have been looked for blind: the landing times stand in before's rows, and both orders in the diff.
- **The start was mis-sized.** Bounds -0.5 to +3.0, taken as 0; the loss to 30 us rose by 3.6. The working ("some 3 us later") was right, and the reason for the zero, that `f` fills what block 3 leaves open, was not. The two rows of the changed kernel:

```profile
10.08 0.61 PE L222 MATMUL tr<-ident,q_t 128*128 128x128 bf16 x4 [0.63 <-DMA q_t<-in_q_dram]
...
20.11 1.14 PE L429 MATMUL hT<-XT,w_in 128*128 128x256 f16 x9
```

Block 1's transposes start at 10.08 instead of 7.16 and the first `f` at 20.11 instead of 17.34: the `f` needs blocks 0 and 1, whose loads stand behind `wi4` as well, so it moved as far as all the rest. In this execution the late start also came with a granted clock of 0.83 over the first 20 us, where before had 1.00; that is at most 0.17 x 20 = 3.4 us, and the runs don't part it from the late loads. Moving `wi4` back by itself (wi4_later, no_moves_start) did not shorten the start, so that `wi4` alone is the cause is not shown.

- **What would have shown it** did: the first `f` later than 18 us, and PE under 96% busy from 40 to 160 (108.6 of 120 us, 91%).
